# Chunked attention, mixture of experts and feed-forward on one core: value transfers of the second half of a batch, with and without the memory rows

## The chip, the core and the metric

The program runs on one core of a Trainium2 chip. Its engines are TensorE (PE for the matmuls, PEld for the weight loads that run beside them), VectorE (DVE), ScalarE (ACT), GpSimd (POOL) and SyncE (SP), which here only issues DMA transfers; sixteen DMA engines move what it issues. The metric is the device time of one execution in microseconds, as the median of several runs. [...]

## What is computed

Three layers follow one another. Only the first is touched by the change. For every chunk of 32 queries it attends to 8 memory rows, which are the same for all chunks of a head, and to a window of 16 + 32 + 8 = 56 keys around the chunk:

```python
k_full = np.concatenate([mem_k, k_ctx], axis=2)   # 8 memory rows and the window
v_full = np.concatenate([mem_v, v_ctx], axis=2)
scores = scale * np.matmul(q_c, k_full.transpose(0, 1, 3, 2))
scores = scores - np.max(scores, axis=-1, keepdims=True)
a = np.exp(scores)
a = a / (np.sum(a, axis=-1, keepdims=True) + 1e-09)
out[:, :, c_start:c_end] = np.matmul(a, v_full)
```

There are 4 batches, 8 heads, 768 positions (24 chunks) and a head width of 64, all in float32. The result, as 3072 rows of 512, goes through a soft mixture of 8 experts (a softmax over all rows, two expert matmuls on 32 slots, a softmax back), and then through a feed-forward layer with a squared ReLU of width 2048.

## The kernel before

**Units.** Attention is cut into 32 units: 4 batches, each in two halves of 12 chunks (`hf` = 0 and 1), each half in 4 pairs of heads (`hp`). The loop at line 460 is written out by hand as a software pipeline: in round `s` it makes the scores of unit `s`, the softmax sums and the transpose of unit `s - 1`, the product with the values (`emit_pv`, line 324) of unit `s - 2`, and issues loads for units ahead. The order in the source is the order on each engine.

**Values.** The array `vm` holds, for each head, 40 rows by 25 blocks of 64 numbers: rows 0 to 31 are a block of 32 positions, and rows 32 to 39 are the 8 memory rows, repeated behind every block. A window with its memory rows is 64 rows deep: 24 late rows of one block with the 8 memory rows (`a` = 0, rows 8 to 39), and all 32 rows of the next block (`a` = 1). `load_v` brings both for two units at once (heads `2*hp` to `2*hp + 3`), in four transfers of 32 rows by 2 heads by 768 numbers: one for each `a` and each `h`, the head's place in its pair. They land in every fourth partition of one of two buffers, `vals0` and `vals1`. Since a half has two such loads, `vals0` always takes heads 0 to 3 and `vals1` heads 4 to 7, and the load of the second half overwrites that of the first half of the same batch, whose memory rows are the same.

**Queue.** All transfers are issued by SP in the order of the source. Eight semaphores go round among them, so an issue also waits until the transfer eight before it has landed. In the attention rounds SP issues the keys and queries (`load_qk`, line 240, 396 KB a unit), the values (line 250, four times 192 KB every second round) and, every second round, 1 MB of expert weights (`load_w`, line 211) for the stage behind attention. A value load also waits for the last product that read its buffer, which is made in the same round.

**Behind attention.** From 111 us on come the softmax over rows, the expert matmuls with `w1` (line 627) and `w2` (line 665), then the feed-forward layer (lines 834, 915 and 927).

Of the kernel before, what the change touches and what calls it, by code (L numbers as in the profile page):

```python
# [18 lines left out]
CH, LC, RC, NM = 32, 16, 8, 8  # L19
# [3 lines left out]
NCU = UT // CH  # L23
# [11 lines left out]
def kernel(  # L35
# [11 lines left out]
    nc = tc.nc  # L47
# [69 lines left out]
    with tc.manual_schedule():  # L117
# [23 lines left out]
        vbuf = [v.rearrange("p (x h c) -> p x h c", x=2, h=2) for v in vals]  # L141
# [91 lines left out]
        def unit(u):  # L233
            g, hp = divmod(u, NHP)
            b, hf = divmod(g, HALF)
            return g, b, hf, hp
# [5 lines left out]
        def load_v(u):  # L242
            g, b, hf, hp = unit(u)
            if u % 2:
                return
            for h in range(2):
                for a in range(2):
                    r0 = 0 if a else LC - RC
                    src = vm[b, 2 * hp + h:2 * hp + 4:2, r0:r0 + CH, hf * NCU + a:hf * NCU + a + NCU, :]
                    nc.sync.dma_start(out=vbuf[u // 2 % 2][2 * h + a:128:4, :, h], in_=src.rearrange("x r c d -> r x (c d)"))  # L250

        def kspread(u):
            g, b, hf, hp = unit(u)
# [178 lines left out]
        load_qk(2)  # L432
        load_w(1)
        load_v(0)
        load_qk(3)
        load_v(2)
        load_qk(4)

# [21 lines left out]
        for s in range(NU):  # L460
# [24 lines left out]
            if s >= 3:  # L485
                when(s + 1, load_v)
# [489 lines left out]
        for k in range(2):  # L976
# [3 lines left out]
                  in_=sot[:, k:k + 1, :, 0:4].to_broadcast([128, 4, 4, 4]))  # L980
# [153 lines left out]
```

## Time and profile before

| what | value |
|---|---|
| median of 3 runs | 469.66 us (468.68 to 470.2) |
| profiled execution | 468.22 us, of which its span 466.4 us |
| PE busy | 448.7 us, 96% of the span |
| ACT, DVE, POOL busy | 298.4, 285.3, 85.4 us |
| bytes moved | 83.03 MB, 178 GB/s over the span |
| chain that ended last | PE 73%, DMA 10%, DVE 7%, ACT 4% |
| transfers issued, added up over part 6 of the page | 171, of which 64 are values |

The profile is one execution. Times are from the span's start. A busy PE is not PE at its peak, since matmuls are pipelined and their ends are modelled. A wait is put down to what came last before it ended; the chain follows these releasers back from the last instruction.

### The profile page before, as it was taken

Reading aid. Unit: us, or ns where it says so; the run is one execution under the profiler, and the core shown is the slowest. Engines: PE = TensorE matmul, PEld = TensorE weight load, DVE = VectorE, ACT = ScalarE, POOL = GpSimd, SP = SyncE. Lnnn points to the kernel's source line nnn. Section 1 sums busy time; section 2 is a strip of 40 time slices with the busy share of each in tenths; the row PEclk is TensorE's granted clock in tenths of the full one; section 3 lists DMA queues with packets and bytes.
Section 4 is the critical chain, followed back from the end, with each engine's and each line's share of the span. In section 5 each row is a group of like instructions: output and inputs, shape, how many; then the busy total and the mean of one; then the engine's idle time right before and its main releaser. Section 6 shows DMA issues by size and latency. Waiting matters only on the chain.

```text
span 466.4 us, 10070 instructions
## 1 busy us (share of the span) xinstructions
PE 448.7 (96%) x3944; PEld 339.3 (73%) x3944; DVE 285.3 (61%) x638; ACT 298.4 (64%) x588; POOL 85.4 (18%) x154
## 2 busy tenths in 40 slices
PE   6799999999999989999999999999999999999996
PEld 5576666665545466888786887888888888888885
DVE  6688888886465768977384989765642242224242
ACT  4476665766225469988686987666666666665670
POOL 6676655561000000000000000000680000000000
PEclk8999999999999999999999999999999999999999
DMA  8999999999999953424222000000320020002011
GB/s 304 400 403 408 406 406 401 395 392 387 410 418 389 417 214 122 151 90 181 90 91 91 0 2 0 1 0 1 144 83 1 0 90 2 0 2 90 1 67 67
DMA packets 20575, 83.03 MB, mean 178 GB/s; under 512 B 2736, under 2 KB 2864, under 8 KB 14640
## 3 DMA queue, kind: packets, MB, share of 16 engines
q1 hardware_dynamic: 20528, 82.39, 45.3%
q8 instruction: 31, 0.51, 0.5%
q14 instruction: 16, 0.13, 0.1%
HBM read 76.09 MB, written 6.29 MB: 177 GB/s over the span
## 4 chain that ended last, share of the span: by engine, by line
PE 73%; DMA 10%; DVE 7%; ACT 4%; POOL 2%; SPq 2%; issue 1%; DVEq 0%; POOLq 0%; ACTq 0%
PE g L915 12%; PE lp L915 6%; PE pt L915 6%; PE g L927 6%; PE xt L915 6%; PE x L915 6%; DMA seg<-in_w_dram 5%; PE s L834 5%; PE s L627 3%; PE pt L927 3%; PE xt L927 3%; PE lp L927 3%; PE x L927 3%; DMA keys<-in_kq_dram 3%; PE x L324 3%; PE s L284 2%
## 5 line engine op out<-in xcount | busy, mean ns | idle before, releaser
L869 DVE TENSOR_TENSOR glo<-vals,ghi 128x512 fp32r<-128x512 f32 x48 | 35.8, 752 | 63.3 <-ACT ghi L865 63.3
L857 ACT ACTIVATE vals<-s 128x512 f32<-128x512 f32 x48 | 28.7, 599 | 45.2 <-PE s L834 45.2
L869 DVE TENSOR_TENSOR glo<-r,ghi 128x384 fp32r<-128x384 f32 x64 | 35.3, 555 | 20.0 <-ACT ghi L865 19.9
L857 ACT ACTIVATE r<-s 128x384 f32<-128x384 f32 x64 | 31.3, 488 | 16.6 <-PE s L834 16.4
L300 ACT ACTIVATE seg<-seg 128x384 f32<-128x384 f32 x32 | 28.8, 901 | 19.0 <-DVE seg L311 15.5
L898 POOL TENSOR_TENSOR keys<-keys,bias 128x512 f32<-128x512 f32 x6 | 8.8, 1496 | 174.0 <-ACT vals L857 174.0
L915 PE MATMUL g<-whi,ghi 128*128 128x512 f32 x126 | 39.6, 391 | 0.3 <-DVE mpack L824 0.3
L927 PE MATMUL g<-wlo,ghi 128*128 128x512 f32 x128 | 39.6, 389 | 0.0
L915 PE MATMUL g<-whi,glo 128*128 128x512 f32 x126 | 39.1, 389 | 0.0
L834 PE MATMUL s<-cpack,mpack 128*128 128x384 f32 (+1 forms) x112 | 37.2, 370 | 0.7 <-ACT r L857 0.4
L861 ACT ACTIVATE r<-r 128x384 f32<-128x384 f32 x64 | 33.7, 527 | 4.7 <-DVE glo L869 2.8
L262 POOL TENSOR_SCALAR keys<-keys 64x416 f32<-64x416 f32 x63 | 33.8, 536 | 10.9 <-DMA keys<-in_kq_dram 6.7
L284 PE MATMUL s<-keys 128*32 128x128 f32 x768 | 29.2, 284 | 5.8 <-POOL keys L266 4.6
L865 ACT CAST ghi<-r 128x384 fp32r<-128x384 f32 x64 | 32.7, 511 | 1.7 <-PE g L927 0.4
L861 ACT ACTIVATE vals<-vals 128x512 f32<-128x512 f32 x48 | 30.4, 634 | 1.8 <-DVE glo L869 0.2
L865 ACT CAST ghi<-vals 128x512 fp32r<-128x512 f32 x48 | 29.9, 622 | 1.5
L324 PE MATMUL x<-vals,seg 128*32 128x128 f32 x744 | 27.7, 275 | 1.6 <-DMA vals<-in_vm_dram 0.9
L324 PEld LDWEIGHTS x<-vals,seg 128*32 128x32 f32 x744 | 20.2, 109 | 12.0 <-DVE seg L308 6.2
L927 PEld LDWEIGHTS g<-wlo,ghi 128*128 128x128 f32 x128 | 24.0, 188 | 5.0
L915 PEld LDWEIGHTS g<-whi,ghi 128*128 128x128 f32 x126 | 23.7, 188 | 5.2 <-DVE mpack L824 0.8
L915 PEld LDWEIGHTS g<-whi,glo 128*128 128x128 f32 x126 | 23.7, 188 | 5.1
L284 PEld LDWEIGHTS s<-keys 128*32 128x32 f32 x768 | 18.9, 111 | 11.6 <-POOL keys L266 7.1
(256 smaller groups left out, 1052.9 us busy)
## 6 DMA issues: line engine op xcount, KB each, us to landing
seg<-in_w_dram SPq DMA_DIRECT2D x27, 1024.0 KB, 8.5
keys<-in_kq_dram SPq DMA_DIRECT2D x32, 396.0 KB, 7.4
vals<-in_vm_dram SPq DMA_DIRECT2D x64, 192.0 KB, 6.5
keys<-in_w_in_dram SPq DMA_DIRECT2D x5, 1024.0 KB, 5.0
keys<-in_w_out_dram SPq DMA_DIRECT2D x5, 1024.0 KB, 5.0
out_dram<-seg SPq DMA_DIRECT2D x18, 256.0 KB, 2.1
vals<-in_w_in_dram SPq DMA_DIRECT2D x3, 1024.0 KB, 6.0
vals<-in_w_out_dram SPq DMA_DIRECT2D x3, 1024.0 KB, 5.0
```

What stands on the lines that cost most here:

```text
L262: (nc.vector if h and u == 0 else nc.gpsimd).tensor_scalar(out=stream(kz[rows, h], 0, CH), in0=k[rows, UT * h:UT * h + (NCU + 1) * CH].rea ...
L284: nc.tensor.matmul(out=o, lhsT=qt[:, 32 * c:32 * c + 32], rhs=kz[:, :, at:at + WIN], start=True, stop=not (first or last))
L300: nc.scalar.activation(out=p_r[u], in_=sm_r[u].rearrange("p t h (a r) -> p t r (h a)", a=2), func=AF.Exp, scale=scale)
L324: nc.tensor.matmul(out=xp[32 * r:32 * r + 32, t], lhsT=pts_r[u][:, 32 * c:32 * c + 32], rhs=vbuf[u // 2 % 2][:, u % 2, :, 64 * c:64 * c + ...
L627: nc.tensor.matmul(out=hp_[32 * e:32 * e + 32, :], lhsT=slotF[:, kc, 4 * eg:4 * eg + 32], rhs=w[:, e, k, :], start=(kc == 0), stop=(kc == ...
L834: nc.tensor.matmul(out=hq, lhsT=mpack[:, 128 * f:128 * f + 128], rhs=cpack[:, 128 * t0:128 * (t0 + nt)], start=True, stop=True)
L857: nc.scalar.activation(out=r_of(n), in_=h_t.pop(n), func=AF.Relu)
L861: nc.scalar.activation(out=r2_of(n), in_=r_of(n), func=AF.Square)
L865: nc.scalar.copy(out=g_of(n)[0], in_=r2_of(n))
L869: nc.vector.tensor_tensor(out=glo, in0=r2_of(n), in1=ghi.bitcast(F32), op=ALU.subtract)
L915: nc.tensor.matmul(out=o_t[r_][t], lhsT=g[x][:, 128 * t:128 * t + 128], rhs=w_hi[f], start=(first and x == 0), stop=False)
L927: nc.tensor.matmul(out=o, lhsT=ghi[:, 128 * t:128 * t + 128], rhs=w_lo[f], start=False, stop=(f == f1 - 1))
```

## The change

In `load_v` the two transfers with `a` = 0 of a load of the second half carry 24 rows, not 32: the 8 memory rows are left out, since the buffer still holds them from the first half. The destination is cut to the same number of rows. The first half's loads, all transfers with `a` = 1, and everything else stay.

```diff
                     r0 = 0 if a else LC - RC
-                    src = vm[b, 2 * hp + h:2 * hp + 4:2, r0:r0 + CH, hf * NCU + a:hf * NCU + a + NCU, :]
-                    nc.sync.dma_start(out=vbuf[u // 2 % 2][2 * h + a:128:4, :, h], in_=src.rearrange("x r c d -> r x (c d)"))
+                    n = CH if a or hf == 0 else CH - NM
+                    src = vm[b, 2 * hp + h:2 * hp + 4:2, r0:r0 + n, hf * NCU + a:hf * NCU + a + NCU, :]
+                    nc.sync.dma_start(out=vbuf[u // 2 % 2][2 * h + a:4 * n:4, :, h], in_=src.rearrange("x r c d -> r x (c d)"))
```

On SP's queue, at the first load that changes (units 4 and 5, the second half of the first batch), a row is a line, what is written and read (`vals_103` is the buffer `vals0`), the shape of one transfer and the semaphores waited for:

```order
-L250 DMA vals_103<-in_vm_dram 32x2x768 [waits DMAHW4_49,PE_49]
-L250 DMA vals_103<-in_vm_dram 32x2x768 [waits DMAHW5_49]
-L250 DMA vals_103<-in_vm_dram 32x2x768 [waits DMAHW6_49]
-L250 DMA vals_103<-in_vm_dram 32x2x768 [waits DMAHW7_49]
+L251 DMA vals_103<-in_vm_dram 24x2x768 [waits DMAHW4_49,PE_49]
+L251 DMA vals_103<-in_vm_dram 32x2x768 [waits DMAHW5_49]
+L251 DMA vals_103<-in_vm_dram 24x2x768 [waits DMAHW6_49]
+L251 DMA vals_103<-in_vm_dram 32x2x768 [waits DMAHW7_49]
```

Two of the four transfers are shorter by a quarter; their number, their places in the queue and their waits are the same. This repeats at 8 of the 16 loads. No instruction of another engine moves. Two later readers of `vals0`, one of ACT (line 578) and one of DVE (line 597), name one more of the eight semaphores, for the transfer that brought the memory rows.

## Rows read from the trace of the kernel before

**Rows 1.** The page, part 2: the span in 40 slices of 11.7 us.

```profile
DMA  8999999999999953424222000000320020002011
GB/s 304 400 403 408 406 406 401 395 392 387 410 418 389 417 214 122 151 90 181 90 91 91 0 2 0 1 0 1 144 83 1 0 90 2 0 2 90 1 67 67
```

**Rows 2.** Stretches: length; busy PE, PEld, DVE, ACT, POOL; clock, DMA share, GB/s.

```profile
17.00:104.00 87.00, 82.76 (x1630) 57.29 (x1622) 72.00 (x218) 56.56 (x122) 54.25 (x115) 1.00 1.02 403
104.00:164.00 60.00, 57.43 (x804) 31.31 (x803) 36.22 (x101) 24.63 (x68) 3.11 (x7) 1.00 1.00 404
164.00:466.40 302.40, 296.94 (x1334) 241.55 (x1330) 166.16 (x285) 209.26 (x391) 18.09 (x12) 1.00 0.16 60
```

**Rows 3.** Waits of PE, 0 to 170 us: waiter, releaser, total us, times, longest.

```profile
PE s L284 <- POOL keys L266: 4.6, 3, 1.8
...
PE x L324 <- DMA vals<-in_vm_dram: 0.9, 1, 0.9
PE xt L665 <- DMA seg<-in_w_dram: 0.7, 2, 0.4
```

**Rows 4.** PE in order of time: start, us, line, operation, [idle before, releaser].

```profile
72.34 0.89 PE L324 MATMUL x<-vals,seg 128*32 128x128 f32 x24 [0.92 <-DMA vals<-in_vm_dram]
...
160.98 1.07 PE L665 MATMUL xt<-seg,seg 128*32 128x256 f32 x16 [0.39 <-DMA seg<-in_w_dram]
...
163.50 0.64 PE L665 MATMUL xt<-seg,seg 128*32 128x256 f32 x8 [0.34 <-DMA seg<-in_w_dram]
```

**Rows 5.** The chain that ended last, from 55 to 73 us: start, us, what.

```profile
55.32 7.38 DMA keys<-in_kq_dram
...
62.76 0.61 SPq L250
...
64.76 7.49 DMA vals<-in_vm_dram
```

**Rows 6.** SP's issues in order of time: start, us, line, transfer, number.

```profile
17.50 2.56 SPq L250 DMA_DIRECT2D vals<-in_vm_dram  x4
...
50.09 2.55 SPq L250 DMA_DIRECT2D vals<-in_vm_dram  x4
...
62.76 2.60 SPq L250 DMA_DIRECT2D vals<-in_vm_dram  x4
...
101.97 2.53 SPq L250 DMA_DIRECT2D vals<-in_vm_dram  x4
```

**Rows 7.** The page, parts 3 and 6: packets, SP's queue, issues of the values.

```profile
DMA packets 20575, 83.03 MB, mean 178 GB/s; under 512 B 2736, under 2 KB 2864, under 8 KB 14640
...
q1 hardware_dynamic: 20528, 82.39, 45.3%
...
vals<-in_vm_dram SPq DMA_DIRECT2D x64, 192.0 KB, 6.5
```

**Rows 8.** Line 250 alone: issue ns min/median/max and first and last start.

```profile
L250 SPq DMA_DIRECT2D vals<-in_vm_dram x64: 598/599/840, 3.9 to 103.9; - x64
...
DMA to landing us min/median/max: 4.3/6.5/7.9
```

**Rows 9.** As rows 2, two stretches with one 1 MB load each.

```profile
184.00:190.00 6.00, 6.00 (x28) 5.04 (x29) 5.90 (x13) 5.87 (x13) 0.00 (x0) 1.00 0.47 180
...
228.00:234.00 6.00, 6.00 (x27) 4.64 (x26) 2.89 (x7) 4.29 (x10) 0.00 (x0) 1.00 0.48 175
```

**Rows 10.** Waits of SP's queue, 17 to 104 us: waiter, releaser, total, times, longest.

```profile
SPq L240 <- DMA seg<-in_w_dram: 12.2, 10, 1.6
SPq L250 <- DMA keys<-in_kq_dram: 6.9, 12, 0.6
SPq L240 <- DMA keys<-in_kq_dram: 5.3, 9, 0.6
SPq L250 <- PE xt L338: 5.2, 8, 1.3
```

## The prediction

> **What bounds the kernel now.** First the slices of the page: the DMA line stands at 9 from the second slice to the fourteenth, some 164 us, and then falls to 0 to 4 [rows 1]. So the kernel has two parts, and the change lies in the first. The busy times by stretch sharpen it: from 17 to 104 us, where all changed transfers are issued, the DMA engines are busy for a share of 1.02 (records overlap a little, so over 1) at 403 GB/s, and from 104 to 164 us, when the expert weights arrive, for 1.00 at 404 GB/s [rows 2]. [...] Transfers and PE are both near their limit. From 164 us on the DMA share is 0.16 and PE has 297 of 302 us: nothing there waits for values.
>
> What one of the two costs the other is read from PE's waits [rows 3]. The largest, 4.6 us on POOL's copies of the keys, belongs to the first 20 us, before any transfer is shortened or when the first has hardly been issued. On a transfer PE waits three times: 0.92 us for values at 72.34 us, and 0.39 and 0.34 us for the last expert weights at 160.98 and 163.50 us [rows 4]. Together that is **1.65 us**. It is all that faster transfers can give back while the work of PE stays as it is.
>
> The chain agrees: before 72 us it runs through a landing of keys at 62.7 us, three issues of SP, a transfer of values from 64.76 to 72.25 us and the product on PE [rows 5]. That load, issued from 62.76 us on, belongs to the first half of a batch and keeps its 32 rows. It can come sooner only if what lies in front of it in the queue is done sooner.
>
> **What the change removes.** In each of 16 transfers (4 batches, 2 pairs of units, 2 heads' places) 8 rows by 2 heads by 768 numbers by 4 bytes: 49,152 of 196,608 bytes. In all that is 0.786 MB of 83.03 MB [rows 7], and at 403 GB/s [rows 2] 1.95 us of all sixteen engines. The number of issues stays 64 [rows 7]. The first shortened load is issued at 17.50 us, the last at 101.97 us [rows 6].
>
> **Whether removed bytes are removed time.** This is the step that decides. A transfer is done when its last engine is done, and the next in an engine's queue starts when that engine is free. So what counts is not the bytes but the bytes on the busiest engine. Before, every transfer has 32 or 128 rows, and the packets under 512 B are 2736, which is 16 for each of the 171 issues: one posting from each engine [rows 7]. So 32 rows lie two on an engine, with two heads each: 4 pieces of 3,072 B. At 403 / 16 = 25.2 GB/s an engine that is 0.49 us a transfer. For 24 rows the trace of before has no row, so the cost is bounded from both sides:
> - evenly over 16 engines, 3 pieces on each: 0.12 us less a transfer, 16 times, the full 1.95 us;
> - two rows on each of 12 engines, 4 pieces: nothing less on these twelve, and 4 engines that do nothing for 0.49 us a transfer;
> - three rows on each of 8 engines, 6 pieces: 0.24 us more a transfer, 3.9 us in all.
>
> I take the middle one: whole rows go to an engine in every transfer that the trace has, in equal numbers, and two rows on each is the load of the nearest one, that of 32 rows [rows 7].
>
> [...]
>
> Could twelve engines be faster because four are silent? A single 1 MB load in the second part moves 180 GB/s at a share of 0.47, and 175 at 0.48, which is 383 and 365 GB/s for a full share [rows 9]; in the crowded part it is 403 / 1.02 = 395 [rows 2]. An engine is not faster when the others rest. I price this at zero.
>
> **Small parts.** An issue of line 250 takes SP 0.599 us in the median and 0.840 at most [rows 8]. If 24 rows took the longer time, SP would spend 16 x 0.24 = 3.9 us more; if they took less, at most a quarter of 0.6 us by the rows, it would be 2.4 us less. Either is hidden: in these 87 us SP waits 24.4 us for landings eight transfers back and 5.2 us for PE on one line alone [rows 10], and a transfer of values lands 6.5 us after its issue [rows 8], so the queue in front of the engines is many times longer than 0.24 us. If that cover were gone, the cost would be at most the three issues in the chain [rows 5], 0.7 us. The memory rows that stay in the buffer add no wait on PE, since they were waited for in the first half; the semaphore that ACT and DVE each name once more in the feed-forward layer stands for a transfer of values, and even the last of these, issued from 101.97 us on [rows 6], has landed after 7.9 us at most [rows 8], long before that layer.
>
> **The sum**: 0 us on the twelve engines, 0 for SP. What is left is the one stall at 72.34 us. If the engine that finished last there is one of the four that now rest, some of its 0.92 us goes; for one engine in four that is 0.2 us on the mean, and I do not count it. The profiled execution took 468.22 us, its 466.4 us of span and 1.8 us around it, and would take 468.2 again. The median of the runs shown is 1.44 us higher, 469.66; I forecast **469.6 us**.
>
> **Rival 1, the bytes count in full.** Sixteen engines share 24 rows evenly, or the limit is the memory and not an engine. By 62.76 us four shortened loads, 8 transfers, lie in front of the load that PE waits for: 8 x 0.12 = 0.98 us, more than the 0.92 us of that wait. By the end all 1.95 us have come in, against 0.92 us that PE has gained and 0.73 us of waits for weights. So all 1.65 us go, and no more: 469.66 - 1.65 = **468.0 us**. For it speaks that the bytes do fall; against it that the transfers of the trace lay whole rows on an engine [rows 7], and that lone transfers are no faster [rows 9]. Chance 0.13.
>
> **Rival 2, fewer and fuller engines.** The place is the same transfer: if 24 rows go to 8 engines, three on each, these carry 0.24 us more at each of the 16 transfers. With the queue at a share of 1.00 to 164 us there is no gap to make it up [rows 2]: the load at 72.34 us comes 8 x 0.24 = 1.95 us later, and the last weights, for which PE already waits at 163.50 us, up to 3.9 us later. That gives **471.6 to 473.5 us**. It decides as soon as an engine gets more than 4 pieces. For it speaks that 8 is a power of two, as 16 is, and no transfer of before shows another count; against it that two rows on each is the present load. Chance 0.10.
>
> **Rival 3, the change does not do what it says** (some transfer still carries 32 rows): SP's order shows 24 rows at 16 transfers, so at most 0.02, at 469.7 us.
>
> **How the numbers follow.** A measurement of this kernel can tell 0.3%, or 1.4 us, from no change. Forecast: 0.72, between 469.0 and 470.4 (the knock-on of shifted landings, some tenths to either side). Rival 1 ends at 1.65 us, just beyond that bound, so two thirds of its chance count as faster and a third as no change. What is left, 0.03, is an issue of SP that gets slower than any row shows. Faster 0.10, no change 0.78, slower 0.12. The range reaches down to rival 1, and up to 470.9 us, the forecast with the 0.7 us of SP's cover and some spread: 468.0 to 470.9 leaves out rival 2 and little else.
>
> **What would show it.** Right: the data moved falls to 82.24 MB, while the DMA share from 17 to 104 us falls by about 0.02 with the same length of the stage; the packets under 512 B fall from 2736 by 16 x 4 = 64 to 2672; the wait at 72 us and those at 161 and 163.5 us stay within some tenths. With rival 1 the small packets stay 2736, and PE's waits for transfers go. With rival 2 they fall to 2608, and the waits for values grow by 2 us and more. The forecast is wrong if the last weights land over 1 us earlier or later than 163.5 us against the start of the span, with the work of PE unchanged.

## The result and the profile after

The changed kernel is slower: **475.58 us** in the median (475.09 to 475.77) against 469.52 us of the kernel before beside it, a ratio of 1.0128 [1.011, 1.0147]. That is 6.06 us, or 0.38 us for each of the 16 shortened transfers. The forecast was 469.6 us in a range up to 470.9. The profiled execution took 475.77 us with a span of 474.0 us, so its difference to the one of before (468.22 us, 1.3 us under the median of its runs) is 7.55 us. Two of the five executions of the kernel `rows24_both` below, 489.96 and 490.73 us, fell in a slower state and are left out of its figures. In the new file all lines behind the edit stand one lower: the values are issued in line 251, the product with them is line 325, the last product with expert weights line 666.

First the page of the changed kernel, to be laid beside [rows 1, 7]: slices of 11.9 us, then the packets.

```profile
DMA  8999999999999992342342000000130010001011
GB/s 314 384 356 400 341 388 357 349 374 323 417 410 389 421 370 88 120 149 90 94 162 100 0 2 0 1 0 1 75 148 1 0 59 31 0 2 73 17 66 66
...
DMA packets 20255, 82.24 MB, mean 174 GB/s; under 512 B 2672, under 2 KB 2800, under 8 KB 14320
```

The edit did what it says: 82.24 MB instead of 83.03, and the small packets fell by 64, which is 4 engines fewer at each of 16 transfers. But the digits of the DMA line stay at 9 for one slice longer, while the rates below them fall to 341, 357, 349 and 323 where before nearly 400 stood. The engines are busy for longer with fewer bytes. (A digit of the DMA line is the busy share of the sixteen engines in tenths, the number below it the GB/s of the same slice.)

Next the stretches of [rows 2] in the changed kernel, and two short ones at the first shortened loads (columns as there).

```profile
17.00:104.00 87.00, 76.30 (x1502) 52.80 (x1494) 66.41 (x197) 51.57 (x109) 51.51 (x109) 1.00 1.01 368
104.00:164.00 60.00, 57.49 (x845) 32.79 (x844) 36.78 (x112) 27.38 (x76) 5.41 (x12) 1.00 1.00 388
...
21.00:24.50 3.50, 3.50 (x81) 2.61 (x75) 3.12 (x9) 2.19 (x4) 3.05 (x7) 1.00 1.06 310
28.50:33.00 4.50, 4.19 (x79) 2.61 (x74) 3.34 (x9) 2.74 (x6) 2.43 (x5) 1.00 1.05 313
34.00:44.00 10.00, 9.67 (x184) 6.43 (x188) 8.13 (x25) 5.46 (x13) 4.47 (x11) 1.00 1.02 397
```

Where a shortened load is under way the queue moves 310 and 313 GB/s, in the kernel before 401 and 406 in the same stretches; between two such loads it moves 397, before 408. The share is 1.02 to 1.06 throughout. So the engines do not stand idle for want of work: they take longer over what they have. The trace's records of single packets say the same. From 28.5 to 33 us a packet of the values (3,072 B) takes 172 ns in the mean, before 127, and one of the 1 MB loads beside them (8,192 B) 408 ns, before 315; from 34 to 44 us they take 128 and 323 ns, before 124 and 319. PE has 6.5 us less work done by 104 us (76.30 against 82.76).

PE's waits in the first 180 us tell where it lost them, beside [rows 3] (waiter, releaser, total us, times, longest).

```profile
PE x L325 <- DMA vals<-in_vm_dram: 6.9, 6, 1.6
PE s L285 <- POOL keys L267: 2.9, 3, 1.4
PE x L325 <- DVE acc L428: 1.8, 2, 0.9
PE xt L666 <- DMA seg<-in_w_dram: 1.1, 2, 0.7
```

The wait for values has grown from 0.9 to 6.9 us. The three longest of the six instances, and the last two waits for expert weights, in order of time (beside [rows 4]):

```profile
34.23 0.86 PE L325 MATMUL x<-vals,seg 128*32 128x128 f32 x24 [1.54 <-DMA vals<-in_vm_dram]
...
76.37 0.86 PE L325 MATMUL x<-vals,seg 128*32 128x128 f32 x24 [1.46 <-DMA vals<-in_vm_dram]
...
91.77 0.86 PE L325 MATMUL x<-vals,seg 128*32 128x128 f32 x24 [1.60 <-DMA vals<-in_vm_dram]
...
168.49 1.07 PE L666 MATMUL xt<-seg,seg 128*32 128x256 f32 x16 [0.73 <-DMA seg<-in_w_dram]
...
171.03 0.64 PE L666 MATMUL xt<-seg,seg 128*32 128x256 f32 x8 [0.36 <-DMA seg<-in_w_dram]
```

The last weights let PE go on at 171.03 us and not at 163.50, 7.53 us later: nearly the whole difference of the spans (474.0 - 466.4 = 7.6 us) stands there, and what follows adds next to nothing. The delay grows over the loads. SP's issues of the changed kernel that answer to [rows 6] (start, us, line, transfer, number):

```profile
17.23 3.12 SPq L251 DMA_DIRECT2D vals<-in_vm_dram  x4
...
52.54 3.04 SPq L251 DMA_DIRECT2D vals<-in_vm_dram  x4
...
108.25 2.98 SPq L251 DMA_DIRECT2D vals<-in_vm_dram  x4
```

The first comes 0.3 us earlier than before, the fourth shortened load 2.45 us later, the eighth 6.28 us later.

### The profile page after: what moved, and what is told of

Read it like the earlier page. It is cut to its first block, busy times and chain, and to the rows that moved or that the text cites. A ratio compares the mean times of both kernels' runs of the same rounds, so it can differ in the third digit from the quotient of the medians.

```text
span 474.0 us, 10071 instructions
## 1 busy us (share of the span) xinstructions
PE 450.6 (95%) x3944; PEld 340.4 (72%) x3944; DVE 285.7 (60%) x638; ACT 297.8 (63%) x588; POOL 85.1 (18%) x154
## 2 busy tenths in 40 slices
DMA packets 20255, 82.24 MB, mean 174 GB/s; under 512 B 2672, under 2 KB 2800, under 8 KB 14320
## 4 chain that ended last, share of the span: by engine, by line
PE 71%; DMA 14%; DVE 6%; SPq 3%; ACT 3%; issue 2%; POOL 1%; DVEq 0%; POOLq 0%; ACTq 0%
PE g L916 12%; DMA vals<-in_vm_dram 8%; PE lp L916 6%; PE pt L916 6%; PE g L928 6%; PE xt L916 6%; PE x L916 6%; DMA seg<-in_w_dram 5%; PE s L835 4%; PE s L628 3%; PE pt L928 3%; PE xt L928 3%; PE lp L928 3%; PE x L928 3%; PE x L325 2%; SPq L251 2%
## 5 line engine op out<-in xcount | busy, mean ns | idle before, releaser
L285 PE MATMUL s<-keys 128*32 128x128 f32 x768 | 30.3, 291 | 3.9 <-POOL keys L267 2.9
```

Of the source, the lines that this page charges most:

```text
L285: nc.tensor.matmul(out=o, lhsT=qt[:, 32 * c:32 * c + 32], rhs=kz[:, :, at:at + WIN], start=True, stop=not (first or last))
```

## The experiments

Two theories were to be told apart. **A**: 24 rows go to 12 engines, and the loss comes from that; a transfer whose rows are divisible by 16 loses nothing. **C**: what counts is how evenly a transfer covers the 128 partitions of its target; a transfer of 32 rows lies on every fourth partition from 0 to 124, one of 24 rows leaves out 96 to 124, so the lower half is used as much as before and the upper half less. (An expectation that has another letter says what it stands for.) The runs of one kernel are compared with runs of the kernel before on the same chip. From experiment 3 on, a loss in us is the ratio given times the median of the kernel before; the difference of the two medians is up to 0.4 us away from it.

**1. Transfers by themselves** (`shapes`). No computation: stretches of 12 transfers with all eight heads (with 24 rows four times the bytes of a shortened transfer of the kernel), with nothing beside them. `rows(n, step)` moves n rows to every `step`-th partition, `full` is a 1 MB load to all 128.

```diff
+phase(lambda j: rows(32, 4))
+phase(lambda j: rows(24, 4))
+phase(lambda j: rows(16, 4))
...
+phase(lambda j: full(j) if j % 2 else rows(32, 4))
+phase(lambda j: full(j) if j % 2 else rows(24, 4))
```

> Attention, experts and feed-forward are all left out; only transfers run, in eleven stretches of 12, each with nothing beside it: 8 heads by n rows by 3,072 B into partitions of a given step. Stretches: 32, 24, 16 and 8 rows at step 4; 24 and 32 rows at step 1; 24 and 32 rows alternating; 1 MB loads of 128 rows; 1 MB alternating with 32, with 24, with 16 rows. Theory A (a row count that 16 does not divide goes to fewer engines, which then get in each other's way): 32 and 16 rows and the 1 MB loads near 400 GB/s, 24 rows clearly under 12/16 of that (under 290 GB/s), with packets longer than those of 32 rows, and the mix with 1 MB loads slower than that without 24. Theory B (four engines rest and nothing else): 24 rows alone at 300 GB/s, packets as long as with 32 rows; the alternation of 24 and 32 and the mix with 1 MB at 340 to 400. Theory C (engines collide on the partitions that they write, whatever their number): 16 rows at step 4 as slow as 24.

The stretches (columns as in rows 2, without PE, PEld and ACT, which do nothing): 32, 24, 16 and 8 rows at step 4, 24 and 32 rows at step 1, then 24 and 32 rows alternating, 1 MB loads, and 1 MB loads alternating with 32, with 24 and with 16 rows.

```profile
47.00:54.00 7.00, 0.46 (x3) 0.00 (x0) 1.00 1.03 401
58.00:80.00 22.00, 0.00 (x0) 0.00 (x0) 1.00 0.78 171
102.00:114.00 12.00, 0.00 (x0) 0.00 (x0) 1.00 1.03 199
125.00:130.00 5.00, 0.00 (x0) 0.00 (x0) 1.00 0.52 206
141.00:166.00 25.00, 0.00 (x0) 0.00 (x0) 1.00 0.78 156
187.00:213.00 26.00, 0.00 (x0) 0.00 (x0) 1.00 1.03 206
234.00:254.00 20.00, 0.00 (x0) 0.00 (x0) 1.00 0.90 249
269.00:284.00 15.00, 0.00 (x0) 0.00 (x0) 1.00 1.01 421
299.00:312.00 13.00, 0.00 (x0) 0.00 (x0) 1.00 1.03 406
329.00:352.00 23.00, 0.00 (x0) 0.00 (x0) 1.00 0.92 226
372.00:384.00 12.00, 0.00 (x0) 0.00 (x0) 1.00 0.97 323
```

24 rows at step 4 move 171 GB/s where 32 rows move 401. The share of 0.78 is that of 12 engines, as the packets of the changed kernel say; twelve engines at the rate of the full row would move 12/16 of 401, 301 GB/s. For a transfer of the kernel (a quarter of these bytes) that is 147,456 B / 171 GB/s = 0.86 us against 196,608 / 401 = 0.49: **0.37 us longer with a quarter fewer bytes**, and 16 x 0.37 = 5.9 us, against the 6.06 us measured. By this row the shape alone would make the whole loss (by the row of the second experiment, 204 GB/s, 3.8 us of it). The expectation's Theory B, 300 GB/s for 24 rows and 340 to 400 with 32 rows in turn (measured 249), is out, and so is Theory A's 400 for 16 rows; only Theory C's, 16 rows as slow as 24, comes near.

The other rows show what lies behind it. 16 rows keep all 16 engines busy (1.03) and move half, 199 GB/s, so engines are not the limit there. 8 rows on half of the engines (0.52) move 206, so an engine is about twice as fast as one of the sixteen in the row above. And 32 rows next to each other (step 1) move 206, 24 of them 156, where 32 rows at step 4 move 401. The rows read from memory are the same whatever the step, so the target sets these rates: 16 and 8 rows at step 4 and 32 at step 1 come to about half of 401. What in the target makes the difference, no run here shows. Beside the slow transfer the 1 MB loads are slow as well: 226 GB/s together against 406. With 16 rows in place of 32 a pair takes as long as before: (1,048,576 + 393,216) B at 323 GB/s are 4.46 us, (1,048,576 + 786,432) B at 406 are 4.52.

**2. More shapes** (`shapes2`), to part engines from partitions; a stretch begins when all transfers of the one before have landed.

```diff
-phase(lambda j: rows(8, 4))
...
+phase(lambda j: rows(28, 4))
+phase(lambda j: rows(24, 5))
+phase(lambda j: rows(12, 4))
+phase(lambda j: rows(16, 8))
+phase(lambda j: rows(16, 4, 64))
+phase(lambda j: full(j, 64, 2), 18)
+phase(lambda j: full(j, 48, 2), 18)
+phase(lambda j: full(j, 96, 1), 18)
+phase(lambda j: full(j, 112, 1), 18)
```

> All computation is left out; only transfers run, in twelve stretches with a wait for all of them in between. Value rows of 8 heads: 32, 28, 24 rows at step 4, 24 at step 5, 12 at step 4, 16 at step 8, 16 at step 4 from partition 64; rows of 8 KB: 64 and 48 at step 2, 96 and 112 at step 1; 1 MB alternating with 24 rows. [...] Theory A: 28 rows at 14/16 and 12 rows at 12/16 of 400 GB/s, 16 rows at step 8 at 400.

In order: 32, 28 and 24 rows at step 4, 24 at step 5, 12 at step 4, 16 at step 8, 16 at step 4 from partition 64; then rows of 8 KB: 64 and 48 at step 2, 96 and 112 at step 1; last 1 MB loads alternating with 24 rows at step 4.

```profile
44.00:64.00 20.00, 0.00 (x0) 0.00 (x0) 1.00 1.03 404
72.00:108.00 36.00, 0.00 (x0) 0.00 (x0) 1.00 0.90 200
116.00:146.00 30.00, 0.00 (x0) 0.00 (x0) 1.00 0.78 204
154.00:178.00 24.00, 0.00 (x0) 0.00 (x0) 1.00 0.77 258
186.00:204.00 18.00, 0.00 (x0) 0.00 (x0) 1.00 0.78 150
212.00:232.00 20.00, 0.00 (x0) 0.00 (x0) 1.00 1.03 195
238.00:258.00 20.00, 0.00 (x0) 0.00 (x0) 1.00 1.04 199
264.00:284.00 20.00, 0.00 (x0) 0.00 (x0) 1.00 1.00 404
294.00:316.00 22.00, 0.00 (x0) 0.00 (x0) 1.00 1.02 248
326.00:372.00 46.00, 0.00 (x0) 0.00 (x0) 1.00 1.01 261
384.00:440.00 56.00, 0.00 (x0) 0.00 (x0) 1.00 1.01 252
452.00:478.00 26.00, 0.00 (x0) 0.00 (x0) 1.00 0.95 283
```

48, 96 and 112 rows are divisible by 16, and all engines are at work (1.01, 1.02); still they move 248 to 261 GB/s where 64 rows move 404. Theory A falls as a full account; none of its numbers in the expectation was met: 28 rows move 200 and not 350 GB/s, 12 rows 150 and not 300, 16 rows at step 8 195 and not 400. 24 rows at step 5 move 258 on as many engines as the 204 at step 4 (share 0.77 and 0.78), and neither comes up to 12/16 of 404, 303. But a wide spread, as C may be read, is not enough either: 16 rows at step 8 lie from partition 0 to 120 and move 195. Of the shapes tried, 32 rows at step 4, 64 at step 2 and all 128 move 401 to 421 by themselves, all others 261 or less. These three go over the whole target in steps of one, two or four partitions. 24 rows at step 4 moved 204 here and 171 in the first row, so its price alone is 0.24 to 0.37 us a transfer of the kernel. Beside 1 MB loads, a pair of (1,048,576 + 589,824) B at 283 and 226 GB/s against (1,048,576 + 786,432) B at 406 is 1.27 to 2.73 us longer; a quarter of that, 0.32 to 0.68 us, is an estimate for a transfer of the kernel.

**3. Half of the rows** (`rows16`): the 16 transfers carry 16 rows. That leaves out 8 rows which are needed, so part of the output is stale; the time stands for what 1.57 MB fewer are worth in a shape that leaves out the upper half of the partitions and keeps 16 engines (2736 small packets on its page, as before).

Against the changed kernel, as in the next two:

```diff
-n = CH if a or hf == 0 else CH - NM
+n = CH if a or hf == 0 else 16
```

> The 16 changed transfers carry 16 rows, not 24: besides the memory rows 8 value rows stay those of the first half, so part of the values is wrong. Theory A (loss from a row count that 16 does not divide): the loss is gone, 467.5 to 469.7 us, 2672 small packets become 2736 again. Theory B (fewer bytes in these transfers let some engines run ahead): 16 rows on 16 engines keep them level, also 467.5 to 469.7. Theory C (collisions on the partitions written): 473 us or more.

Measured: 471.68 us against 470.41, 1.0023 [1.0004, 1.0043]. Twice the bytes left out bring nothing. That lies between the expected times, 467.5 to 469.7 us by Theories A and B and 473 or more by C, and meets neither. From 17 to 104 us it reads:

```profile
17.00:104.00 87.00, 80.73 (x1594) 56.02 (x1597) 70.09 (x210) 55.21 (x119) 53.87 (x113) 1.00 1.02 380
```

The engines are as busy as before at 380 GB/s. By the first experiment 16 rows take (98,304 B / 199 GB/s) 0.49 us, as long as 32. The kernel, 1.1 us slower in all, is close to that.

**4. The change in both halves** (`rows24_both`), so 32 shortened transfers; the memory rows are then never loaded, so the output is not the right one.

```diff
-n = CH if a or hf == 0 else CH - NM
+n = CH if a else CH - NM
```

> The first half of a batch leaves out the 8 memory rows as well, so that they count as zero values: 32 transfers of 24 rows instead of 16. Theory A: the loss goes by the number of such transfers, 6.1 us for 16, so about 481 us (479 to 483). Rival (the loss belongs to the second half only, for instance to the rows that stay in the buffer): about 475.6 us.

Measured: 1.0284 [1.0264, 1.0305], 13.4 us, 0.42 us a transfer. Twice the transfers, a little over twice the loss; the rival, a loss of the second half alone, is out.

**5. 28 rows** (`rows28`), half of the change's saving, no issue more.

```diff
-n = CH if a or hf == 0 else CH - NM
+n = CH if a or hf == 0 else 28
```

> The kernel before, but the 16 transfers that the change touches carry 28 of their 32 rows (half of the bytes that the change leaves out; the 4 rows left out are mem rows that stand in the buffer, so nothing that is computed changes). No issue is added. Theory C (the shape sets the price): in the second row of transfers alone, 28 rows at step 4 moved 200 GB/s where 32 moved 404, so one transfer of 172,032 B takes 0.86 us and not 0.49: 16 x 0.37 = 6 us longer, ratio 1.0128, so as long as the changed kernel although it leaves out half as many bytes. Rival (a loss for each row left out): half of the changed kernel's 6.06 us, ratio 1.0065. Rival (bytes): a gain of at most 1 us.

Measured: 478.44 us against 470.33, 1.0176 [1.0156, 1.0195], 8.3 us or 0.52 us a transfer. So the kernel that leaves out fewer rows loses **more** than the changed one, [1.011, 1.0147]. No account by bytes or by missing rows gives that. The shapes do as to the sign and most of the size, with 200 GB/s for 28 rows, 0.86 us against 0.49; but that is 0.37 us, and 0.52 were measured. Two things may make the rest, and no run parts them. Beside 1 MB loads the price may be higher, as the estimate for 24 rows is. And in the profiled execution the granted clock (a share of full speed) was 0.72 from 36 to 42 us and again from 94 to 100 us, just after PE had waited 2.40 and 2.10 us for values; that takes up to 1.7 us of PE's work each time (0.28 x 6). In the changed kernel's profiled execution it was 1.00 all through this part. The page shows 14 engines (2736 - 2704 = 2 x 16), and PE waits for values longer than in the changed kernel:

```profile
DMA packets 20415, 82.64 MB, mean 173 GB/s; under 512 B 2704, under 2 KB 2832, under 8 KB 14480
...
PE x L325 <- DMA vals<-in_vm_dram: 8.1, 6, 2.4
```

**6. The same bytes left out evenly** (`cols9`): all 32 rows, but 9 of 12 chunks of each, so 0.786 MB fewer, as in the change. Three chunks of values are stale, and part of the output with them. (The source is cut to the same 9 chunks, not shown here.)

```diff
+w = NCU if a or hf == 0 else 9
...
-nc.sync.dma_start(out=vbuf[u // 2 % 2][2 * h + a:128:4, :, h], ...)
+nc.sync.dma_start(out=vbuf[u // 2 % 2][2 * h + a:128:4, :, h, 0:64 * w], ...)
```

> The kernel before, but the 16 transfers that the change touches keep all 32 rows and carry 9 of the 12 chunks of a head (so the same 0.786 MB fewer as in the changed kernel, taken evenly from all 32 rows; three chunks of values stand from an earlier batch half, which leaves part of the output wrong). Theory C (what counts is how evenly a transfer covers the 128 partitions and the 16 engines): bytes left out in an even shape are left out in time, at most 16 x 49,152 B / 403 GB/s = 1.95 us, of which PE can take back at most 1.65 us: ratio 0.996 to 1.000, no loss. Rival (any transfer whose shape differs from the others, or the smaller bytes as such, disturb the stream): a loss of several us, ratio 1.01. The wait of PE for values in the first 180 us stays at about 1 us under C, and is near 7 us under the rival.

Measured: 468.87 us against 469.96, 0.9978 [0.9956, 0.9999]: 1.0 us faster, with an interval from nothing to 2.1 us. Stretch and wait:

```profile
17.00:104.00 87.00, 83.64 (x1648) 58.03 (x1640) 72.88 (x219) 56.64 (x121) 53.64 (x114) 1.00 1.02 400
...
PE x L325 <- DMA vals<-in_vm_dram: 0.7, 1, 0.7
```

So 49,152 B fewer in an even shape are a small gain at most, and in the change's shape a loss of 6 us. The bytes are not the cause, nor is it that 16 transfers differ from the others.

**7. Splitting by rows** (`split24_8`, `split16_16`, `split16_8`). The 16 transfers are cut in two by rows: 24 + 8 and 16 + 16 with the bytes of the kernel before, 16 + 8 with those of the change.

```diff
+for p0, p1 in ((0, CH),) if a or hf == 0 else ((0, 24), (24, CH)):   # or (0, 16), (16, CH); or (0, 16), (16, 24)
+    src = vm[b, 2 * hp + h:2 * hp + 4:2, r0 + p0:r0 + p1, hf * NCU + a:hf * NCU + a + NCU, :]
+    nc.sync.dma_start(out=vbuf[u // 2 % 2][4 * p0 + 2 * h + a:4 * p1:4, :, h], ...)
```

> The bytes of the kernel before, but each of the 16 transfers in two pieces, of 24 rows and of the 8 memory rows: 16 issues more. Theory A: the 24-row piece costs what it costs in the changed kernel, and the 8-row piece adds to it, 476 to 480 us. Rival (the loss comes from rows that are no longer written, or from what waits for them): 469 to 471 us.

> The bytes of the kernel before; each of the 16 transfers in two pieces of 16 rows, every one divisible by 16, 16 issues more. [...] Theory A (only a row count that 16 does not divide costs): no change, ratio 1.000 to 1.003 with the issues.

> The bytes of the changed kernel, the memory rows left out of the second half, but the 24 rows in pieces of 16 and 8. Theory C: 0.49 us for 16 rows and 0.24 us for 8 (0.95 us for 8 heads) against 0.49 us for the 32 rows of before: 16 x 0.24 = 3.8 us more than before, ratio 1.008, and 2 us less than the changed kernel. Theory A: 8 rows go to 8 engines as 24 go to 12, so as slow as the changed kernel, ratio 1.013. If only the bytes counted: 1.65 us less than before, ratio 0.9965.

Measured: 24 + 8 is 480.26 us against 470.41, 1.0218 [1.0201, 1.0235], 10.25 us; 16 + 16 is 476.53 against 470.26, 1.0125 [1.0092, 1.0157], 5.9 us; 16 + 8 is 475.87 against 470.26, 1.012 [1.0093, 1.0147], 5.6 us. At first sight the 16 + 16 spoke for C: by the first experiment a piece of 16 rows takes 0.49 us by itself, as long as all 32, so two pieces would cost 16 x 0.49 = 7.8 us more. Neither that estimate nor Theory A's 0 was met. All three also add 16 issues, and that needed a control.

**8. The control: splitting by heads** (`split_heads`): the same bytes in two transfers of one head and 32 rows each.

```diff
+for x in ((0, 2),) if a or hf == 0 else ((0, 1), (1, 2)):
+    src = vm[b, 2 * hp + h + 2 * x[0]:2 * hp + 2 * x[1]:2, r0:r0 + CH, ...]
+    nc.sync.dma_start(out=vbuf[u // 2 % 2][2 * h + a:128:4, x[0]:x[1], h], ...)
```

> The kernel before, but each of the 16 transfers that the change touches is issued as two, of one head each, with all 32 rows (the same bytes in the same places, 16 more issues). A control for the runs that split by rows. Theory C: each half covers the partitions as the whole did, so only the extra issues on SP can cost: ratio 1.000 to 1.003 (0 to 1.5 us). Rival (it is the extra issue and completion that cost in the kernels split by rows, not their rows): as much as the kernel of 16 + 16 rows lost, 5.9 us, ratio 1.0125.

Measured: 475.67 us against 469.96, 1.0115 [1.0081, 1.0149], 5.4 us. My expectation was wrong: the split costs 5.4 us with no change of shape. So **the times of 16 + 16 and 16 + 8 tell nothing of the shape**: their 5.9 and 5.6 us are no more than the split. C's price of 7.8 us for 16 + 16 falls too: two halves that use opposite partitions and are in the queue together lose nothing beyond the split that the intervals could tell, though their packets of values take 142 ns in the mean from 17 to 104 us, against 129 with the split by heads. Only 24 + 8 says more: 10.25 - 5.4 = 4.8 us, 0.30 us for each of the 16, lie beyond the split, give or take 1.8 us by the two intervals. (In the profiled executions the granted clock fell to 0.72 over 6 us in both, twice with 24 + 8 and once with the split by heads, so up to 1.7 us of the difference may be that.)

The split loses in another way than the change. Around 52 us of the split by heads (two stretches, then the SP queue's issues before it and its largest wait of line 251 from 17 to 164 us):

```profile
51.40:54.60 3.20, 3.00 (x59) 1.92 (x48) 3.14 (x13) 2.19 (x5) 0.93 (x3) 1.00 0.70 221
17.00:51.00 34.00, 29.63 (x597) 20.89 (x589) 25.02 (x73) 20.11 (x41) 21.52 (x45) 1.00 1.00 384
...
46.24 5.06 SPq L251 DMA_DIRECT2D vals<-in_vm_dram  x6
...
SPq L251 <- DMA seg<-in_w_dram: 7.5, 6, 1.9
```

SP needs 5.06 us for the six issues of a load, 2.55 us for four before [rows 6], and then the engines run out of work, with a share of 0.70. In the changed kernel, read in stretches of 3 us from 17 to 110 us, the share stays between 0.95 and 1.06. Each issue waits until the transfer eight before it has landed, so with smaller transfers fewer bytes are under way; that this and SP's time per issue empty the queue is read from these rows, and was not tried by itself.

## Why the prediction was wrong

- **What bounds the kernel**: held. The queue is full (a share of 1.01 and 1.00) to the end of the expert weights, and a delay in it reaches the end unshortened: the 7.53 us at the last weights are nearly all of the difference of the profiled executions.
- **Bytes, issues, engines**: held. 0.786 MB fewer, 64 issues of values (48 with 192 KB and 16 with 144 KB), and two rows on each of 12 engines, by the packets and by the share of 0.78 in shapes. The middle case of the three, two rows on an engine, was the right one, and with 28 rows it was the same (14 engines, 2704 small packets).
- **The price of that case is the step that failed.** It was set to 0, from the sentence that what counts is "the bytes on the busiest engine". That takes an engine's time as fixed by its own bytes, at 25.2 GB/s. The same transfers by themselves show +0.24 to +0.37 us for an unchanged load of each busy engine, the kernel +0.38. Rows 9 did show that lone 1 MB loads are no faster; but those go to all 128 partitions, as the keys and weights in the queue of before do, and its values go to every fourth of them. So the profile of before has no transfer of 24 rows, and could not show that beside one a packet of the values takes 172 ns instead of 127. "I price this at zero" bounded the term from the side of gains only; a loss from packets that take longer had no bound, and it belongs beside the case of 8 engines. The prediction's own sign of being wrong came: the last weights let PE go on at 171.03 us, not within 1 us of 163.5.
- **Rival 2** came out on the right side and for the wrong reason: its time, 471.6 to 473.5 us, rests on 0.24 us more for three rows on an engine. The engines carry two rows, and its marker (2608 small packets) did not appear; its other marker, waits for values that grow by 2 us and more, did (6 us).
- **Rival 1** asked what the bytes are worth. In the even shape of `cols9` they are worth 1.0 us, within the at most 1.65 us that PE could take back. So that part of the sum agrees with the run, for a change that this one is not. (By the stated parts the chances were 0.09 faster and 0.13 slower, not 0.10 and 0.12, which changes nothing.)
- **SP's small parts**: an issue of line 251 took a median of 608 ns and 922 at most, against [rows 8]; a shortened load's four issues took 3.0 to 4.2 us. So SP spent some 0.45 us more on a shortened load than the 2.55 us of before, near the longer time that the prediction allowed for. It is not the cause by the share, which would have fallen with an empty queue, as it did in the split, and stayed at 0.95 and above; and 24 rows are as slow in `shapes`, where a transfer takes 3.4 us and an issue of SP 0.8. `cols9` does not test it, since its loads took SP 2.6 us.
- **What stays open**: what in the target sets the rate of a shape. In proportion to the rows 24 would move 24/32 of 404, 303 GB/s, and 28 rows 354; measured were 171 to 204 and 200. (12 rows, 150, and 16 rows, 199, are near this proportion: 152 and 202. 8 rows, 206, are at twice theirs.) The packet records of `shapes2` narrow it. With 32 rows at step 4, 99% of the packets take at most 135 ns; with 24 rows at step 4 31% do and 49% take 200 ns or more; with 24 rows at step 5 it is 63% and 13%. So the slow transfers are a mix of packets as fast as before and packets of 200 ns and more. Why a part of them is slow, why 24 rows at step 5 are faster than at step 4 on as many engines, and which row goes to which engine, no run here shows.

No version was found that is faster than both kernels. `cols9` suggests that some 1 us is to be had if the bytes go evenly, but it leaves out values that are needed; the memory rows are the last 8 of 32 and lie on one side, and to spread them the rows of keys and values would have to be laid out in another order. That was not tried.

## What to carry to other kernels

Before rows are cut from a transfer, measure the shape that is left: by themselves 32 rows at step 4 moved 401 and 404 GB/s, 24 rows 171 and 204, 28 rows 200 and 16 rows 199, and in the full queue of this kernel 24 rows cost 6.06 us, 28 rows 8.3 us, and 16 rows, with half of the bytes, gained nothing (1.1 us slower). Cut along the free dimension (the numbers within a partition) instead, which was 1.0 us faster in `cols9`, or leave the bytes in. And cutting a transfer in two is not free either where eight may be under way at a time: here it cost 0.34 us for each transfer that was cut.

## What the runs showed that I had not expected

- 28 of 32 rows move 200 GB/s, fewer than half of the 404 of all 32; 112 of 128 rows of 8 KB move 252 against 421 for a full 1 MB.
- Transfers of 24 rows slow what stands beside them: 1 MB loads with 24 rows between them move 226 and 283 GB/s together, with 32 rows 406; in the changed kernel a packet of a 1 MB load beside a shortened one took 408 ns instead of 315.
- 16 of 32 rows take as long as all 32, by themselves (199 and 401 GB/s) and beside 1 MB loads (4.46 and 4.52 us a pair).
- 16 more issues of transfers half as large cost 5.4 us in a stretch where SP waits a good deal [rows 10].
